# Attention in couples of query groups by Strassen's seven block products, with array halves that swap PSUM banks

## The chip, the cores and the metric

The kernel runs on one core of one Trainium2 chip. The metric is the device time of one execution in microseconds (us); lower is better. Every kernel was run several times, each time beside runs of the kernel before on the same chip. On one core a run is put down as slow when it is over 1.5% above the fastest of the same kernel; only fast runs are compared here. Profiled spans are some 2 us shorter than the device time of the same run.

In the profile PE is TensorE, PEld its weight loads, DVE VectorE, ACT ScalarE, POOL GpSimd and SP SyncE. "SPq" is SP's sequencer, which issues the DMA transposes. L199 is line 199 of the kernel named.

## The reference, cut to what matters

```python
# u, v: (8, 3072, 256), z: (8, 3072, 64); w1, w2: (256, 1024), w_out: (1024, 256)
scores = z @ z^T / 3072                     # symmetric
x      = u * (max(scores, 0) ** 2 @ v)      # per batch
g      = maximum(x @ w1, x @ w2)
out    = g @ w_out                          # float32
```

A batch has 24 tiles of 128 tokens. The kernels work on groups of four tiles (512 queries), so a batch has six groups and its squared-relu matrix is 6 by 6 blocks of 512 by 512. The matrix is symmetric: a block above the diagonal is computed, the one below is its transpose, made by a DMA transpose ("mirror").

## The kernel before

One query group's attention is 48 steps: 24 key tiles times two halves of the output width. Each step is two matmuls of 64 rows by 512 columns, one in each half of the array. Each half adds into a bank of its own, and the two banks are merged afterwards (`drain`).

```python
def attn_unit(b, g, t, acc, dc, first, last):          # one step
    blk, j = divmod(t, G)
    a = A[b, g, blk]
    for half in range(2):
        rows = ds(half * R, R)                         # R = 64
        ...                                            # (cut: natural or mirrored block)
        nc.tensor.matmul(o, v_sb[b][rows, t, ts(dc, P)], mv, start=first, stop=last)

def drain(acc, dcs):                                   # merge the halves
    ...
        nc.scalar.copy(hs[dc], acc[1, dc])
    for dc in dcs:
        nc.vector.tensor_add(hs[dc], hs[dc], acc[0, dc])

def mirror(b, g, blk):                                 # block below the diagonal
    t = tpool.tile([P, G, G, P], bf16, name="at_sb")
    nc.sync.dma_start_transpose(t..., A[b, g, blk]...)
    A[b, blk, g] = t

def turn_u(b, g):
    t = upool.tile([P, G, KD, P], bf16, name="uT")
    nc.sync.dma_start_transpose(t..., un[b, g]...)     # z likewise (zT)

def gate(b, g, hs):                                    # DVE: xT = c2 * h * uT, two of 128x512
    ...

def ff1(xT, g_sb):
    for nb in range(KF):                               # eight slices of the first projection
        ...                                            # two matmuls into d_ps
        if nb % 2 == 0:
            nc.scalar.activation(g_sb[:, nb, :], d_ps, AF.Relu)
        else:
            nc.vector.tensor_single_scalar(out=g_sb[:, nb, :], in_=d_ps, scalar=0.0, op=ALU.max)
```

The feed-forward has been folded beforehand: max(a, b) = b + relu(a - b), so one projection with w1 - w2 and a product with w2·w_out are left. Attention and feed-forward of two groups alternate on TensorE.

Of the kernel before, what the change touches and what calls it, by code (L numbers as in the profile page):

```python
# [11 lines left out]
def kernel(  # L12
# [25 lines left out]
    NG = NT // G  # L38
    KD = D // P
    KF = Dff // P  # L40
    AHEAD = 11
    c2 = float((1.0 / S) * (1.0 / S))


    consts = ctx.enter_context(tc.tile_pool(name="consts", bufs=1))
    znat = ctx.enter_context(tc.tile_pool(name="znat", bufs=1))
    zpool = ctx.enter_context(tc.tile_pool(name="zpool", bufs=2))
    vpool = ctx.enter_context(tc.tile_pool(name="vpool", bufs=2))
    unat = ctx.enter_context(tc.tile_pool(name="unat", bufs=2))
    upool = ctx.enter_context(tc.tile_pool(name="upool", bufs=3))  # L50
    apool = ctx.enter_context(tc.tile_pool(name="apool", bufs=11))
    tpool = ctx.enter_context(tc.tile_pool(name="tpool", bufs=13))
    rpool = ctx.enter_context(tc.tile_pool(name="rpool", bufs=3))
    hpool = ctx.enter_context(tc.tile_pool(name="hpool", bufs=4))
    xpool = ctx.enter_context(tc.tile_pool(name="xpool", bufs=4))
    gpool = ctx.enter_context(tc.tile_pool(name="gpool", bufs=2))
# [8 lines left out]
    zn, zd, zT, v_sb, un, uT = {}, {}, {}, {}, {}, {}  # L65

    def load_z(b, lo, n, held=False):
        if b not in zn:
            zn[b] = znat.tile([P, NT, dqk], bf16, name="zn")
            zd[b] = znat.tile([P, NT, 2, dqk], bf16, name="zd")  # L70
            zT[b] = zpool.tile([P, NT, P], bf16, name="zT")
        sl = ds(lo, n)
        if held:
            nc.vector.memset(zn[b][:, lo, 0:1], 0.0)
        nc.gpsimd.dma_start(out=zn[b][:, sl, :], in_=by_tile(z[b])[:, sl, :])

    def first_z(lo, n):

        if 0 not in zd:
            zd[0] = znat.tile([P, NT, 2, dqk], bf16, name="zd")  # L80
            zT[0] = zpool.tile([P, NT, P], bf16, name="zT")
        t = tpool.tile([P, n, dqk], fp32, name=f"z32_{lo}", tag="at_sb")
        nc.sync.dma_start(out=t, in_=by_tile(z[0])[:, ds(lo, n), :])
        return t

    def double_first(t, lo, n, at=0, copies=None):
        for copy, h in zip(copies or (nc.vector.tensor_copy, nc.scalar.copy), range(2)):
            copy(zd[0][:, ds(lo, n), h, :], t[:, ds(at, n), :])

    def double_z(b, lo, n):  # L90
        sl = ds(lo, n)
        for h in range(2):
            nc.vector.tensor_copy(zd[b][:, sl, h, :], zn[b][:, sl, :])

    def zT_dma(b):
        nc.sync.dma_start_transpose(zT[b], zd[b].rearrange("p t h d -> p (t h d)"))

    def zT_pe(b, lo, n, engine):
        tp = mm_psum.tile([P, n, P], bf16, name="tpz", tag="mm")
        for j in range(n):  # L100
            nc.tensor.transpose(
                tp[:, j, :], zd[b][:, lo + j, :, :].rearrange("p h d -> p (h d)"), ident
            )
        copy = nc.scalar.copy if engine == "act" else nc.vector.tensor_copy
        copy(zT[b][:, lo : lo + n, :], tp)

    def load_v(b, lo, n, held=False):
        if b not in v_sb:
            v_sb[b] = vpool.tile([P, NT, D], bf16, name="v_sb")
        sl = ds(lo, n)  # L110
        if held:

            nc.vector.memset(v_sb[b][:, lo, 0:1], 0.0)  # L113
        nc.gpsimd.dma_start(out=v_sb[b][:, sl, :], in_=by_tile(v[b])[:, sl, :])  # L114
# [12 lines left out]

    A = {}
    later = []
    whole_first = (0, NG - 1)  # L130
    V_ORDER = (1, 2, 3, 4, 5, 0)
    V_LATE = [(3, 14), (4, 8), (4, 14), (5, 2), (5, 8), (5, 14)]

    def score_pair(b, g, m, dve_half=None, halves=False):
        blk = m // 2
        if m % 2 == 0:
            A[b, g, blk] = apool.tile([P, G, GW], bf16, name="a_sb")
        a = A[b, g, blk]
        k = 2 * (m % 2)

        triangle = blk == g and whole_first < (b, g)
        lo = [(k + h) * P if triangle else 0 for h in range(2)]
        s_ps = []
        for h in range(2):
            rows = ds(h * R, R)
            s_ps.append(mm_psum.tile([P, GW], fp32, name="s_ps", tag="mm"))
            nc.tensor.matmul(  # L147
                s_ps[h][:, lo[h] :],
                zT[b][rows, 2 * m + h, :],
                zT[b][rows, g * G + lo[h] // P : g * G + G, :].rearrange("p t c -> p (t c)"),  # L150
                start=True,
                stop=True,
            )
# [7 lines left out]
        if halves or triangle:  # L161
            for h in range(2):
                o = r[:, h, lo[h] :]
                nc.vector.tensor_mul(a[:, k + h, lo[h] :], o, o)  # L164
        else:
            nc.vector.tensor_mul(a[:, k : k + 2, :], r, r)  # L166
        if triangle and m % 2 == 1:
            for j in range(G - 1):
                nc.sync.dma_start_transpose(
                    a[:, j + 1 :, ts(j, P)], a[:, j, (j + 1) * P :]  # L170
                )
        if m % 2 == 1 and blk > g:
            if b == 0 and g < 2 and blk > 2:
                later.append((b, g, blk))
            else:
                mirror(b, g, blk)

    def mirror(b, g, blk):

        t = tpool.tile([P, G, G, P], bf16, name="at_sb")  # L180
        nc.sync.dma_start_transpose(
            t.rearrange("p k j r -> p (k j) r"),
            A[b, g, blk].rearrange("p k q -> p (k q)"),
        )
        A[b, blk, g] = t



    def attn_unit(b, g, t, acc, dc, first, last):
        blk, j = divmod(t, G)  # L190
        a = A[b, g, blk]
        for half in range(2):
            rows = ds(half * R, R)
            if blk >= g:
                o, mv = acc[half, dc], a[rows, j, :]
            else:
                o = acc[half, dc].rearrange("p (k r) -> p k r", r=P)
                mv = a[rows, :, j, :]
            nc.tensor.matmul(o, v_sb[b][rows, t, ts(dc, P)], mv, start=first, stop=last)  # L199

    def drain(acc, dcs):
        hs = {}
        for dc in dcs:
            hs[dc] = hpool.tile([P, GW], fp32, name="h_sb")
# [5 lines left out]
    def drain_fast(acc, dc):  # L210

        hs = [hpool.tile([P, GW], fp32, name="h_sb") for half in range(2)]
# [3 lines left out]

    def gate(b, g, hs):
        xT = xpool.tile([P, KD, GW], bf16, name="xT")
        for dc in range(KD):
            nc.vector.scalar_tensor_tensor(  # L220
                out=xT[:, dc, :].rearrange("p (t r) -> p t r", r=P),
# [6 lines left out]
        return xT  # L228

    def ff1(xT, g_sb):  # L230
        for nb in range(KF):
# [9 lines left out]
            if nb % 2 == 0:  # L241
                nc.scalar.activation(g_sb[:, nb, :], d_ps, AF.Relu)  # L242
            else:
# [3 lines left out]

    def ff2(b, g, xT, g_sb, last=False):
        dst = by_tile(out[ds(b * S, S), :])[:, ds(g * G, G), :]
        o_sb = opool.tile([P, G, D], fp32, name="o_sb")  # L250
        for t0 in range(0, G, 2):
            o_ps = mm_psum.tile([P, 2, D], fp32, name="o_ps", tag="mm")
            for t in range(2):
# [16 lines left out]
            nc.scalar.copy(o_sb[:, t0 : t0 + 2, :], o_ps)  # L270
            if last:
                nc.sync.dma_start(out=dst[:, ds(t0, 2), :], in_=o_sb[:, t0 : t0 + 2, :])
        if not last:
            nc.sync.dma_start(out=dst, in_=o_sb)
# [7 lines left out]


    def ff_follows(i):
        return i >= 2 and i % 2 == 0 or i == len(groups) - 1

    def edge(i):

        return 0 if ff_follows(i) else 4 if i < 2 else 9
# [9 lines left out]
    def pair_slots(i):  # L299
        if i == 0:  # L300
            return [1, 3] + list(range(6, 40, 4))
        if i == 1:
            return list(range(3, 41, 4))
        if ff_follows(i):
            return [3, 9, 15, 21, 26, 31, 36, 40]
        return [0, 5, 10, 15, 20, 25, 30, 41]



    groups = [(b, g) for b in range(B) for g in range(NG)]  # L310

    def tiles_of(b, g):
        own = list(range(g * G, g * G + G))
        rest = list(range(g * G + G, NT))
        return list(range(g * G)) + (own + rest if (b, g) <= whole_first else rest + own)

    pairs, need = [], {}
    for i, (b, g) in enumerate(groups):
        order = [(b, g, m) for m in range(2 * g, NT // 2)]
        base = len(pairs)  # L320
        pairs += order
        most = base
        for n, t in enumerate(tiles_of(b, g)):
            if t // G >= g:
                most = max(most, base + order.index((b, g, t // 2)) + 1)
            need[i, n] = most

    done = 0

    def ahead(upto):  # L330
        nonlocal done
        while done < min(upto, len(pairs)):
            early = done < 22
            score_pair(
                *pairs[done],
                dve_half=1 if early and done % 3 == 0 else None,
                halves=done == 0,
            )
            done += 1

    def ff(prev):
        g_sb = gpool.tile([P, KF, GW], bf16, name="g_sb")
        ff1(prev[2], g_sb)
        return g_sb

    with tc.manual_schedule():
        z32a = first_z(0, 4)
        z32b = first_z(4, 8)
        z32c = first_z(12, 12)
        warm = consts.tile([P, GW], bf16)  # L350
# [156 lines left out]
```

## Time and profile before

| | before |
|---|---|
| device time | 969.06 us (968.63 to 970.68, 3 runs) |
| profiled span | 966.4 us |
| attention, all stretches on TensorE | 583.5 us |
| feed-forward, all stretches on TensorE | 377.8 us |
| one batch, steady | 118.2 us |
| attention of two groups, steady | 24.17, 23.96 or 22.88 us, mean 23.67 |
| feed-forward of two groups | 15.75 us |

The stretches are worked out from the start times of the matmuls in the trace: a stretch runs from its first matmul to the first one of the other kind.

The page of the kernel before has these lines (busy us and share by engine; busy tenths in 40 slices for PE and the DMA engines; the chain that ended last; two groups, with busy us and mean ns of one; block transposes with the median us from issue to landing):

```profile
PE 954.8 (99%) x7994; PEld 621.6 (64%) x8042; DVE 487.2 (50%) x847; ACT 557.6 (58%) x1058; POOL 61.0 (6%) x118
...
PE   8999999999999999999999999999999999999998
...
DMA  9999798988689976999869988699967998767611
...
PE 96%; DVE 1%; issue 1%; ACT 1%; DMA 1%; DVEq 0%; POOLq 0%
...
L244 DVE TENSOR_SCALAR g_sb<-d_ps 128x512 bf16<-128x512 f32 x192 | 132.8, 692 | 146.1 <-PE d_ps L234 146.1
...
at_sb<-a_sb SPq DMA_TRANSPOSE x120, 5.0
```

TensorE is busy 99% of the span and is 96% of the chain; DVE idles half of the time. TensorE's longest waits, from the waits view (us in total, times, longest):

```profile
PE acc_134 L374 <- DVE warm L351: 1.2, 1, 1.2
PE acc_427 L199 <- DVE a_sb L166: 1.1, 3, 0.5
```

There is nothing longer than 1.2 us in the whole run. The windows view of the start (length, busy us of PE, PEld, DVE, ACT and POOL, then granted clock, DMA share, GB/s) reads:

```profile
0.00:60.00 60.00, 54.97 (x465) 27.82 (x467) 40.67 (x68) 41.73 (x75) 12.59 (x27) 1.00 1.10 182
60.00:100.00 40.00, 39.90 (x338) 24.03 (x338) 22.15 (x39) 25.88 (x49) 2.65 (x5) 1.00 1.11 199
100.00:160.00 60.00, 59.84 (x506) 37.31 (x508) 27.69 (x49) 33.91 (x65) 3.71 (x7) 1.00 0.86 152
```

After the first 60 us TensorE is never short of work. A DMA share of 1 or just over it is to be read as "full".

### The profile page before, as it was taken

How to read it: one execution, taken by the hardware profiler on the slowest of the kernel's cores; microseconds unless marked ns; L12 is line 12 of the kernel's file. 1: busy time of each engine (PE TensorE's matmuls, PEld its weight loads, DVE VectorE, ACT ScalarE, POOL GpSimd, SP SyncE). 2: the span in 40 equal slices, each digit the busy share in tenths (PEclk: the TensorE clock that was granted, in tenths of full speed). 3: DMA queues.
4: the chain of work that ended last, by engine and by line, in shares of the span. 5: the costliest groups of instructions: out<-in, count | busy, mean ns of one | idle time of the engine just before them, and what ended most of it. 6: DMA issues, size and time to landing. Idle time of an engine off the chain costs nothing.

```text
span 966.4 us, 19478 instructions
## 1 busy us (share of the span) xinstructions
PE 954.8 (99%) x7994; PEld 621.6 (64%) x8042; DVE 487.2 (50%) x847; ACT 557.6 (58%) x1058; POOL 61.0 (6%) x118
## 2 busy tenths in 40 slices
PE   8999999999999999999999999999999999999998
PEld 4465667675666756667566765676756776566655
DVE  6746454463555534555346553464545554445433
ACT  6757466563575645756456564565556656466433
POOL 3001000100000000000000000000000000000000
PEclk9999999999999999999999999999999999999999
DMA  9999798988689976999869988699967998767611
GB/s 186 186 207 175 135 156 158 179 149 166 134 140 188 146 157 126 164 185 148 150 133 146 184 152 160 131 162 176 150 141 140 157 170 168 135 131 145 124 56 44
DMA packets 382296, 145.99 MB, mean 151 GB/s; under 512 B 360832, under 2 KB 361984, under 8 KB 382208
## 3 DMA queue, kind: packets, MB, share of 16 engines
q1 hardware_dynamic: 365792, 115.25, 62.5%
q0 software_dynamic: 16416, 29.50, 20.8%
q8 instruction: 63, 1.03, 0.4%
q14 instruction: 25, 0.20, 0.1%
HBM read 59.77 MB, written 25.17 MB: 88 GB/s over the span
## 4 chain that ended last, share of the span: by engine, by line
PE 96%; DVE 1%; issue 1%; ACT 1%; DMA 1%; DVEq 0%; POOLq 0%
PE o_ps L263 17%; PE d_ps L234 17%; PE s_ps L147 7%; PE o_ps L255 4%; DMA v_sb<-in_v_dram 1%; DVE a_sb L166 1%; PE acc_12604 L199 1%; PE acc_6354 L199 1%; PE acc_4771 L199 1%; PE acc_3187 L199 1%; PE acc_11103 L199 1%; PE acc_9519 L199 1%; PE acc_7936 L199 1%; PE acc_1582 L199 1%; PE acc_1581 L199 1%
## 5 line engine op out<-in xcount | busy, mean ns | idle before, releaser
L199 PEld LDWEIGHTS <-v_sb 64*128 64x128 bf16 x4608 | 314.6, 94 | 181.4 <-issue 5.9
L160 ACT ACTIVATE r_sb<-s_ps 128x512 bf16<-128x512 f32 (+3 forms) x664 | 333.8, 555 | 90.4 <-PE s_ps L147 88.8
L166 DVE TENSOR_TENSOR a_sb<-r_sb 128x1024 bf16<-128x1024 bf16 x251 | 173.6, 692 | 243.0 <-ACT r_sb L160 239.0
L244 DVE TENSOR_SCALAR g_sb<-d_ps 128x512 bf16<-128x512 f32 x192 | 132.8, 692 | 146.1 <-PE d_ps L234 146.1
L263 PE MATMUL o_ps<-w_out_sb,g_sb 128*128 128x256 bf16 x1536 | 199.1, 273 | 0.0
L234 PE MATMUL d_ps<-xT,w_sb 128*128 128x512 bf16 x720 | 167.4, 379 | 2.6 <-issue 0.2
L263 PEld LDWEIGHTS <-g_sb 128*128 128x128 bf16 x1536 | 150.2, 98 | 20.8
L242 ACT ACTIVATE g_sb<-d_ps 128x512 bf16<-128x512 f32 x192 | 114.8, 598 | 82.0 <-PE d_ps L234 57.1
L147 PE MATMUL s_ps<-zT 64*128 64x512 bf16 (+3 forms) x672 | 148.6, 357 | 0.9 <-DVE r_sb L158 0.5
L270 ACT COPY o_sb<-o_ps 128x512 f32<-128x512 f32 x96 | 56.3, 586 | 150.3 <-PE o_ps L263 149.2
L234 PEld LDWEIGHTS <-w_sb 128*128 128x128 bf16 x768 | 73.2, 98 | 89.6 <-issue 9.8
L255 PE MATMUL o_ps<-W2o_sb,xT 128*128 128x256 bf16 x384 | 73.3, 273 | 0.0
L118 POOL DMA_DIRECT2D un<-in_u_dram x48 | 25.7, 537 | 731.2 <-DMA uT<-un 717.6
L147 PEld LDWEIGHTS <-zT 64*128 64x128 bf16 x672 | 47.6, 94 | 29.0 <-issue 4.6
L220 DVE SCALAR_TENSOR_TENSOR xT<-h_sb,uT 128x512 bf16<-128x512 f32 x96 | 61.8, 685 | 0.0
L164 DVE TENSOR_TENSOR a_sb<-r_sb 128x512 bf16<-128x512 bf16 (+3 forms) x170 | 47.9, 323 | 14.7 <-ACT r_sb L160 14.5
L255 PEld LDWEIGHTS <-xT 128*128 128x128 bf16 x384 | 37.6, 98 | 14.1
L114 POOL DMA_DIRECT2D v_sb<-in_v_dram x48 | 25.8, 546 | 59.1 <-DVE v_sb L113 58.3
L199 PE MATMUL acc_134<-a_sb,v_sb 64*128 64x512 bf16 x24 | 8.7, 377 | 0.5 <-DMA v_sb<-in_v_dram 0.4
L199 PE MATMUL acc_136<-a_sb,v_sb 64*128 64x512 bf16 x24 | 8.7, 378 | 0.0
L199 PE MATMUL acc_137<-a_sb,v_sb 64*128 64x512 bf16 x24 | 8.5, 376 | 0.0
L199 PE MATMUL acc_135<-a_sb,v_sb 64*128 64x512 bf16 x24 | 8.5, 376 | 0.0
(577 smaller groups left out, 1665.3 us busy)
## 6 DMA issues: line engine op xcount, KB each, us to landing
out_dram<-o_sb SPq DMA_DIRECT2D x47, 512.0 KB, 4.0
v_sb<-in_v_dram POOLq DMA_DIRECT2D x48, 256.0 KB, 7.0
un<-in_u_dram POOLq DMA_DIRECT2D x48, 256.0 KB, 5.0
zn<-in_z_dram POOLq DMA_DIRECT2D x7, 384.0 KB, 6.7
a_sb<-a_sb SPq DMA_TRANSPOSE x126, 2.7
at_sb<-a_sb SPq DMA_TRANSPOSE x120, 5.0
uT<-un SPq DMA_TRANSPOSE x48, 3.3
w_132<-in_moe_w_dram POOLq DMA_DIRECT2D x1, 512.0 KB, 5.1
```

Source lines behind the costliest of these rows:

```text
L147: nc.tensor.matmul(s_ps[h][:, lo[h] :], zT[b][rows, 2 * m + h, :], zT[b][rows, g * G + lo[h] // P : g * G + G, :].rearrange("p t c -> p (t ...
L160: nc.scalar.activation(o, s, AF.Relu)
L164: nc.vector.tensor_mul(a[:, k + h, lo[h] :], o, o)
L166: nc.vector.tensor_mul(a[:, k : k + 2, :], r, r)
L199: nc.tensor.matmul(o, v_sb[b][rows, t, ts(dc, P)], mv, start=first, stop=last)
L220: nc.vector.scalar_tensor_tensor(out=xT[:, dc, :].rearrange("p (t r) -> p t r", r=P), in0=hs[dc].rearrange("p (t r) -> p t r", r=P), scala ...
L234: nc.tensor.matmul(d_ps, w15_sb[:, kc, ts(nb, P)], xT[:, kc, :], start=(kc == 0), stop=(kc == KD - 1),)
L242: nc.scalar.activation(g_sb[:, nb, :], d_ps, AF.Relu)
L244: nc.vector.tensor_single_scalar(out=g_sb[:, nb, :], in_=d_ps, scalar=0.0, op=ALU.max)
L255: nc.tensor.matmul(o_ps[:, t, :], xT[:, dc, ts(t0 + t, P)], W2o_sb[:, dc, :], start=(dc == 0), stop=False,)
L263: nc.tensor.matmul(o_ps[:, t, :], g_sb[:, nb, ts(t0 + t, P)], w_out_sb[:, nb, :], start=False, stop=(nb == KF - 1),)
L270: nc.scalar.copy(o_sb[:, t0 : t0 + 2, :], o_ps)
```

## The change

Two query groups become a couple; a batch has three couples. For the blocks of a couple that lie off the couple's diagonal, the 2 by 2 block product (two query groups by two key groups, times two key groups by two halves of v's width) is done with Strassen's seven products (in Winograd's form) for eight. The couple's own four blocks are done plainly. That is 7 x 8 + 4 x 8 = 88 steps for a couple where 2 x 48 = 96 stood. Four forms of A and four of v are needed: S1 to S4 are sums of whole 128x2048 blocks, the forms of v smaller.

A bank now holds one product, with both halves of the array added into it: the halves work on different products, and swap. An order between the halves is kept by no-ops on POOL (the prediction's relays). So nothing is merged, but the products have to be added up (U2, U3, V), on DVE.

In batch 0 the first four groups stay plain (`PLAIN = 4`), so 22 couples take the new form. The core of the diff, with cuts marked `...`:

```diff
+    PLAIN = 4
...
-    apool = ctx.enter_context(tc.tile_pool(name="apool", bufs=11))
-    tpool = ctx.enter_context(tc.tile_pool(name="tpool", bufs=13))
+    free = [apool.tile([P, G * GW], bf16, name=f"blk{n}") for n in range(NSLOTS)]   # 27
-    hpool = ctx.enter_context(tc.tile_pool(name="hpool", bufs=4))
+    hpool = ctx.enter_context(tc.tile_pool(name="hpool", bufs=5))
...
+    def prepare(b, c):                       # DVE: three block sums for each of two couples
+        ...
+                nc.vector.tensor_add(f["S1"].ap, f["A21"].ap, f["A22"].ap)
+                nc.vector.tensor_sub(f["S2"].ap, f["S1"].ap, f["A11"].ap)
+                nc.vector.tensor_sub(f["S3"].ap, f["A11"].ap, f["A21"].ap)
+    ORDER = (                                # what each half of the array works on, in turn
+        (("P1", "P6", "P7", "X11"), ("X11", "P1", "P6", "P7")),
+        (("D22", "X12", "P5", "X21"), ("P5", "X21", "D22", "X12")),
+    )
+    BANK = {"P1": 0, "P6": 1, "P7": 2, "X11": 3, "D22": 0, "P5": 1, "X21": 2, "X12": 3}
...
-            if nb % 2 == 0:
-                nc.scalar.activation(g_sb[:, nb, :], d_ps, AF.Relu)
-            else:
+            if nb in (2, 5, 7):
                 nc.vector.tensor_single_scalar(...)
+            else:
+                nc.scalar.activation(g_sb[:, nb, :], d_ps, AF.Relu)
+            hook(1, nb)                      # DVE tasks are put between the relus
...
-        if not last:
-            nc.sync.dma_start(out=dst, in_=o_sb)
+            nc.scalar.copy(o_sb, o_ps)       # two stores of 256 KB for one of 512
+            nc.sync.dma_start(out=dst[:, ds(t0, 2), :], in_=o_sb)
...
+    return forms, list(gates) + sums[:3] + tasks + sums[3:]     # order of DVE's tasks
...
+                (50, lambda: turn_u(b, q1)),                     # u of a couple, at steps 50 and 60
+                (60, lambda: turn_u(b, q2)),
...
+                    if (s, half) in marks:
+                        relay = nc.gpsimd.nop()
+                        tc.add_manual_dep(relay.ins, mm.ins.name, AFTER, reason="half done")
```

All off-diagonal blocks of both groups of a couple must be there, in their mirrored form where they lie below the diagonal, before the couple's block sums can be made. And the gates of the couple just attended stand first in the list of DVE's work for the feed-forward that follows, which is that of the couple before it.

## The prediction

> **What bounds the kernel now.** TensorE. The page's busy table gives PE 99%, against ACT 58% and DVE 50% of a 966.4 us span; the chain of waits is 96% PE; the granted clock is 1.000. In the timeline, the feed-forward of two groups takes 15.75 us, the attention of two groups 22.9 to 24.2 us, and each couple of half-array matmuls (64 rows, 512 columns, one in each half) starts 0.2155 us after the last. Sum per batch: 118.25 us, of which 3 x 96 x 0.2155 = 62.1 us are attention products, 8.9 us scores, 47.25 us feed-forward. The Trainium skill, "TensorEngine Tiling (Array Packing)", Key Properties, says that row tiles run independently; the trace agrees, as two matmuls of 0.38 us start within 0.01 to 0.11 us of each other.
>
> **What the change removes.** Off the diagonal, seven products replace eight: 88 steps per couple of groups instead of 96, in 22 couples (the first four groups of batch 0 stay plain). 22 x 8 x 0.2155 = 37.9 us of TensorE, all on the critical path. ACT evictions of accumulators fall from 88 to 44; one relu of eight goes from DVE to ACT.
>
> **What it adds.** DVE, per couple: eight sums of 128x2048 bf16 (the one in the trace took 1.219 us; about 1.13 start to start, estimated from 0.60 for 1024), eight 512-wide fp32 additions where four were (0.60 us start to start), and about four 512-wide V sums (0.34). Per batch I estimate 46 us of DVE issue in the attention stretches and 46 in the feed-forward, 92 of about 114 us: 81%, from some 45%. DMA work stays (share 0.85 to 0.9 in the windows table). The half-swap relays through POOL have at least eight steps (1.7 us) of slack, so they should cost nothing; two halves never write one bank at once, as the same skill page's Gotcha 1 demands (no run here tests that).
>
> **What is given back.** In the feed-forward DVE is as loaded as TensorE. After attention, DVE first does two final additions and a gate before the first relu that ff1 needs, and the third relu comes late for the second projection: an estimated 0.3 us of TensorE wait per couple, and 0.3 more in one couple of three where a 1.2 us block sum stands between relus of the second group. That is some 9 us over the run, in place of nearly none now. The plain start and DVE queueing behind transposes: 3 to 5 us more.
>
> **Predicted time:** 969 - 38 + 13 = 944 us, 8 in 10 between 935 and 960. Chances: faster by over 2% 0.69, within 2% 0.28, slower 0.03.
>
> **What would show it.** 176 steps of two matmuls fewer (7994 recorded matmuls down by about 350); attention stretches of two groups 1.7 us shorter; feed-forward stretches 16.0 to 16.6 us instead of 15.75, the gap before the second projection released by a DVE relu; DVE busy near 80%; PE still above 97% and the chain of waits still mostly PE; steps of two matmuls still 0.2155 us apart.
>
> **What would make it wrong.** DVE's queue runs later than I think (block sums waiting for transposes that read the block they overwrite, gates waiting for the u transpose), so that attention waits for sums or relus: 960 or more. Half-array matmuls of different products failing to overlap (steps over 0.22 us) would cancel the gain. If DVE's slack suffices everywhere, 935.

## More of the kernel before

All transposes stand in one stream, SP's, in program order. They have to: the Trainium skill, "DMA: Bandwidth & Descriptors", section "Silent corruption: two transposing streams in flight at once", says that two streams whose transposes are in flight together can corrupt each other's output. No run here tests that; both kernels and every experiment keep to it.

## The result, and the profile after

| | before | after |
|---|---|---|
| device time, median | 968.88 us (968.63 to 970.68, 4 runs) | 955.26 us (954.55 to 955.75, 4 runs) |
| profiled span | 966.4 us | 952.7 us |
| attention, all stretches | 583.5 us | 556.2 us |
| feed-forward, all stretches | 377.8 us | 391.6 us |
| one batch, steady | 118.2 us | 113.9 us |
| attention of a couple, steady | mean 23.67 us | 21.48, 22.12, 21.80, mean 21.80 us |
| feed-forward of a couple, steady | 15.75 us | 15.96 us mostly, up to 17.07 |

The ratio is 0.9856 (95% interval 0.9842 to 0.987). Here and below a ratio is the mean time of one kernel's fast runs over that of the other's of the same rounds, so not quite the ratio of the medians quoted. The changed kernel is 1.4% faster: inside the predicted range, 11 us above its centre, and in the class "within 2%" that the prediction held for less likely. All results were correct.

The page after:

```profile
PE 926.9 (97%) x7690; PEld 519.1 (54%) x7690; DVE 731.9 (77%) x1180; ACT 551.9 (58%) x1062; POOL 57.2 (6%) x111
...
PE   8968979999999999999999999999999999999998
...
DMA  9998996989898897887958989689899989884401
...
PE 89%; DMA 4%; DVE 4%; SPq 1%; issue 1%; ACT 1%; DVEq 0%; ACTq 0%; POOLq 0%
...
L403 DVE TENSOR_SCALAR g_sb<-d_ps 128x512 bf16<-128x512 f32 x144 | 96.2, 684 | 27.1 <-PE d_ps L395 23.3
...
L311 DVE TENSOR_TENSOR blk<-blk,blk 128x2048 bf16<-128x2048 bf16 x44 | 53.8, 1223 | 1.3
...
blk<-blk SPq DMA_TRANSPOSE x246, 5.0
```

DVE went from 50% to 77%. (The 246 transposes are 120 of blocks and 126 of triangles of diagonal blocks, as before, where they have two names. The median of 5.0 us is of both kinds here; in the trace the 120 of blocks alone have 6.0 us, against 5.0 in the kernel before.) The row of slices shows where TensorE is not full: the third, the fourth and the sixth, that is, before 143 us. The waits view of TensorE agrees:

```profile
PE s_ps L201 <- DMA zT<-zd: 9.1, 1, 9.1
PE d_ps L395 <- DVE g_sb L403: 4.6, 3, 3.9
PE s_ps L201 <- ACT o_sb L431: 1.7, 2, 1.3
...
PE o_ps L423 <- DVE g_sb L403: 0.8, 4, 0.2
```

Three waits that the kernel before doesn't have stand out, and the longest case of each (9.1, 3.9 and 1.3 us) lies in the start. The windows view of the changed kernel cuts the run there:

```profile
60.00:64.60 4.60, 4.60 (x44) 2.18 (x40) 3.44 (x7) 4.60 (x10) 0.00 (x0) 1.00 0.82 180
64.60:73.70 9.10, 0.03 (x2) 0.00 (x0) 1.25 (x4) 0.27 (x1) 0.53 (x1) 0.65 1.05 199
73.70:78.70 5.00, 4.96 (x28) 1.69 (x28) 1.40 (x3) 2.27 (x5) 1.59 (x3) 0.62 1.13 210
60.00:163.50 103.50, 88.66 (x717) 49.15 (x714) 72.92 (x122) 58.66 (x116) 5.84 (x11) 0.93 0.92 160
163.50:882.50 719.00, 716.72 (x5990) 401.70 (x5990) 584.35 (x941) 422.77 (x820) 38.15 (x72) 1.00 0.90 159
```

From 163.5 us on TensorE is busy 716.7 of 719 us. Between 60 and 163.5 us it is busy 88.7 of 103.5 us, and it also runs slower after the two longer holes: the clock granted was 0.65 in the hole of 9.1 us and 0.62 in the 5 us after it. By the Trainium skill, "TensorE: Matmul & The Clock Gate", Part 1, about 3.4 us of idleness bring the clock to half and about 3.4 us of work bring it back. The trace agrees in size: the clock is at half from 67.26 to 77.50 us, that is, from 2.6 us after the last matmul's end until 3.8 us after work goes on, and again from 125.29 to 128.70 us, after the second hole; the third and shortest hole has no such stretch. So the two longer holes cost more than their length.

**The first hole** (64.6 to 73.7 us). The chain of waits of the changed kernel, in this window alone, shows what TensorE waited for (start us, us, what):

```profile
63.55 0.24 PE s_ps L201 x2
63.79 0.72 SPq L243
...
64.61 2.01 SPq L177
...
66.72 3.60 SPq L243
...
70.42 3.27 DMA zT<-zd
...
73.74 0.61 PE s_ps L201 x2
74.35 1.71 PE acc L259 x5
```

The last plain group has finished batch 0's scores, and its slots emit two pairs of score matmuls of batch 1. These need batch 1's z, turned. The transpose (L133) stands behind a transpose of u (L177) and block transposes (L243) in SP's stream. From 35.87 to 64.5 us SP issues nine block transposes, one every 3.2 us, without a pause. TensorE has work of batch 0 ready but works in program order.

**The second hole** (120.8 us, 4.25 us without a matmul start; this feed-forward takes 21.50 us instead of 15.75). DVE's lines in the timeline (start, length, idle before it and its releaser):

```profile
123.69 0.69 DVE L379 SCALAR_TENSOR_TENSOR xT<-h_sb,uT 128x512 bf16<-128x512 f32 x1 [3.69 <-DMA uT<-un]
124.29 0.68 DVE L403 TENSOR_SCALAR g_sb<-d_ps 128x512 bf16<-128x512 f32 x1
```

The gate waits for u, turned by a transpose that was issued at 115.61 and landed only at 123.66 us, between block transposes issued at 113.13 and 117.31 us. The relu that TensorE needs stands behind the gate on DVE.

**The third hole** (141.2 to 143 us). A score matmul needs a PSUM bank which ACT empties; ACT waits for an output buffer. Its store was ready when ACT's copy, begun at 129.5 us, had ended; SP issued it at 138.18 us, after block transposes at 129.58, 131.63 and 136.36 us, and it landed at 142.19 us. ACT's waits of this kind in the whole run (the longest, 6.9 us, is this one; the six others come later):

```profile
ACT o_sb L431 <- DMA out_dram<-o_sb: 21.2, 7, 6.9
```

The sum of it, all from the stretches. Twenty-two couples at 1.87 us less (23.67 - 21.80) should take 41.1 us from attention; it lost 27.3 us. The missing 13.8 us lie in the plain start (12.8 us longer than in the first experiment, which takes the first hole away) and in the couple with the third hole (2.2 us over its steady 21.80); these come to 15.0 us, so the other stretches won 1.2 us more than the count. The feed-forward grew by 13.9 us: 6.2 us in its first two stretches (16.16 and 21.50), 7.7 us in all the others together. So the start gave back about 20 us, the steady feed-forward about 8.

### The profile page after: what moved, and what is told of

Same layout as the page of the kernel before. It is cut to its first block, busy times and chain, and to the rows that moved or that the text cites. A ratio compares the mean times of both kernels' runs of the same rounds, so it can differ in the third digit from the quotient of the medians.

```text
span 952.7 us, 19447 instructions
## 1 busy us (share of the span) xinstructions
PE 926.9 (97%) x7690; PEld 519.1 (54%) x7690; DVE 731.9 (77%) x1180; ACT 551.9 (58%) x1062; POOL 57.2 (6%) x111
## 2 busy tenths in 40 slices
DMA packets 388651, 145.99 MB, mean 153 GB/s; under 512 B 361936, under 2 KB 365904, under 8 KB 388560
## 4 chain that ended last, share of the span: by engine, by line
PE 89%; DMA 4%; DVE 4%; SPq 1%; issue 1%; ACT 1%; DVEq 0%; ACTq 0%; POOLq 0%
PE acc L789 44%; PE o_ps L423 17%; PE d_ps L395 15%; PE s_ps L201 6%; PE o_ps L415 4%; PE acc L259 3%; DMA uT<-un 2%; DVE g_sb L403 1%; DVE blk L303 1%; DVE blk L222 1%; DMA blk<-blk 1%; SPq L243 1%; DVE xT L379 1%; DMA v_sb<-in_v_dram 1%; DMA out_dram<-o_sb 0%
## 5 line engine op out<-in xcount | busy, mean ns | idle before, releaser
L789 PE MATMUL acc<-blk,v_sb 64*128 64x512 bf16 x2464 | 465.4, 376 | 0.0
L789 PE MATMUL acc<-blk,vt 64*128 64x512 bf16 x1408 | 345.0, 376 | 0.0
L789 PEld LDWEIGHTS <-v_sb 64*128 64x128 bf16 x2464 | 182.9, 94 | 136.5 <-issue 4.6
L222 DVE TENSOR_TENSOR blk<-r_sb 128x1024 bf16<-128x1024 bf16 x251 | 170.8, 689 | 106.4 <-ACT r_sb L214 104.8
L789 PEld LDWEIGHTS <-vt 64*128 64x128 bf16 x1408 | 131.4, 94 | 74.0 <-issue 0.6
L201 PE MATMUL s_ps<-zT 64*128 64x512 bf16 (+3 forms) x672 | 126.9, 358 | 11.6 <-DMA zT<-zd 9.1
L706 DVE TENSOR_TENSOR h_sb<-h_sb,acc 128x512 f32<-128x512 f32 x154 | 101.5, 682 | 28.7 <-PE acc L789 27.9
L403 DVE TENSOR_SCALAR g_sb<-d_ps 128x512 bf16<-128x512 f32 x144 | 96.2, 684 | 27.1 <-PE d_ps L395 23.3
L220 DVE TENSOR_TENSOR blk<-r_sb 128x512 bf16<-128x512 bf16 (+3 forms) x170 | 50.7, 323 | 35.1 <-ACT r_sb L214 34.2
L259 PE MATMUL acc<-blk,v_sb 64*128 64x512 bf16 x384 | 52.1, 385 | 2.9 <-DVE blk L222 1.2
L311 DVE TENSOR_TENSOR blk<-blk,blk 128x2048 bf16<-128x2048 bf16 x44 | 53.8, 1223 | 1.3
L307 DVE TENSOR_TENSOR blk<-blk,blk 128x2048 bf16<-128x2048 bf16 x44 | 53.6, 1217 | 0.0
```

Of the source, the lines that this page charges most:

```text
L201: nc.tensor.matmul(s_ps[h][:, lo[h] :], zT[rows, z_at(b, blk * G + tiles[h]), :], zT[rows, q + lo[h] // P : q + G, :].rearrange("p t c -> ...
L222: nc.vector.tensor_mul(a[:, k : k + 2, :], r, r)
L259: nc.tensor.matmul(a.out(acc[half, dc]), v_at(b, t, dc)[rows], a.moving(rows, j), start=first, stop=last,)
L706: nc.vector.tensor_add(out, a, b_)
L789: mm = nc.tensor.matmul(a.out(acc[name]), w()[rows], a.moving(rows, j), start=name not in opened, stop=left[name] == 0,)
```

## The experiments

Three theories stood at the outset. By the first, the three holes are three separate mistakes of order, and each one taken away gives its length back. By the rival (B, called the transposes in flight, their bandwidth, or the amount of DMA work), the delivery of the transposes limits the start: what waits changes when a wait is taken away, not when they come. By a third, DVE's order in the feed-forward (gates and sums before relus) is what costs, and it should be changed for all batches. Where the expectations use letters for theories, they say beside them what each expects. The first four kernels ran on one chip with one set of runs of the kernel before (median 968.66 us).

### 1. No scores of batch 1 in the plain start

```diff
-                while done < min(upto, len(pairs)):
+                while done < min(upto, per_batch):
```

> Edit: the plain start emits score pairs of batch 0 only, so TensorE does not stop at 64.6 us for the z transpose of batch 1. Theory A (a score pair placed too early waits in order for a transpose that stands behind others in the SP queue): the 9.1 us hole and the half-clock stretch after it (5 us at granted clock 0.62) vanish, 943 to 948 us against 955.3. Rival B (the transposes in flight are the limit, so TensorE only waits elsewhere, at the block sums or the u gates): the hole is gone but waits after it grow, 951 to 955 us.

Measured: 958.52 us (953.97 to 962.49), ratio 0.9895 (0.9861 to 0.9929). The first hole is gone and the plain stretch is 64.70 us instead of 77.52. But the next two feed-forward stretches took 21.17 and 27.41 us. TensorE's waits:

```profile
PE d_ps L395 <- DVE g_sb L403: 13.4, 5, 5.3
PE s_ps L201 <- ACT o_sb L431: 2.2, 2, 1.9
```

The attention of batch 1's first couple begins at 138.03 us, against 139.47 in the changed kernel, so 1.4 of 12.8 us are kept at that point, and the median is no better. The windows view of this kernel:

```profile
60.00:100.00 40.00, 36.30 (x290) 20.60 (x290) 28.80 (x53) 23.79 (x49) 2.64 (x5) 0.96 1.01 170
100.00:160.00 60.00, 48.82 (x393) 28.61 (x393) 40.69 (x65) 31.33 (x64) 2.64 (x5) 0.94 0.82 147
```

The time went over to the gates that wait for u. (The profile is of the fastest of the four runs.) Between 100 and 160 us the DMA share is 0.82 while TensorE idles, so the bytes that the DMA engines can move are not the whole limit.

### 2. The first couple's u turned first

```diff
+        for q in range(2):
+            load_u(0, PLAIN + q)
...
-                (50, lambda: turn_u(b, q1)),
-                (60, lambda: turn_u(b, q2)),
+                (0 if early else 50, lambda: turn_u(b, q1)),     # early: the first couple alone
+                (0 if early else 60, lambda: turn_u(b, q2)),     # (its loads at steps 2 and 6 fall away)
```

> Edit: in the first couple by seven products (batch 0) the two u transposes are issued at its first step instead of steps 50 and 60, ahead of the block transposes in the SP queue. Theory A (queue order: the gates wait for u transposes that were issued last): the 3.9 us hole in the feed-forward at 121 us and the half clock after it vanish, 949 to 951 us. Rival B (transpose bandwidth): the wait moves to the output writes or the block sums, 954 to 955.5 us.

Measured: 955.5 us (953.42 to 956.62), ratio 0.9863 (0.9848 to 0.9877). The second hole is gone (that feed-forward takes 16.39 us). The third has grown:

```profile
PE s_ps L201 <- DMA zT<-zd: 9.2, 1, 9.2
PE s_ps L201 <- ACT o_sb L431: 6.3, 1, 6.3
```

The feed-forward after batch 1's first couple begins at 165.28 us, against 163.46 in the changed kernel.

### 3. Both

The edits of 1 and 2 together.

> Edit: both of the foregoing. Theory A: 937 to 942 us, the two savings add up and the steady batches (113.9 us each) stay as they are. Rival B: what is saved at the start is lost again before the third couple, 948 us or more.

Measured: 953.54 us (950.0 to 959.13), ratio 0.9842 (0.9795 to 0.9889). The first feed-forward has a hole of 8.33 us (a transpose of u landed 12.1 us after its issue), and a wait for the store takes 9.0 us. That feed-forward begins at 165.93 us.

### 4. Batch 1's first z turned early

```diff
-                if (i, n) in ((2, 6), (2, 20)):
+                if (i, n) in ((1, 6), (2, 20)):        # load
-                if (i, n) in ((3, 4), (3, 8)):
-                    turn_z(1, int(n == 8))
+                if (i, n) in ((2, 2), (3, 8)):         # transpose
+                    turn_z(1, int(i == 3))
```

> Edit: the early score pairs of batch 1 stay, but the z piece that they read is loaded and transposed a group and a half earlier, so that its transpose stands before some six block transposes in the SP queue. Theory A (order in the queue, not the amount of work): the 9.1 us hole goes, 943 to 949 us. Rival B (amount of work): the block transposes pushed back by it hold TensorE instead, 952 us or more.

Measured: 957.55 us (947.64 to 961.11), ratio 0.987 (0.9815 to 0.9925). The wait for z is gone; in its place, in TensorE's waits:

```profile
PE d_ps L395 <- DVE g_sb L403: 11.1, 2, 10.7
PE s_ps L201 <- ACT o_sb L431: 4.0, 4, 2.2
PE acc L259 <- DMA blk<-blk: 3.9, 1, 3.9
```

What follows from 1 to 4: each edit removed the wait it was made for, and none moved the median by more than 4 us. Whichever waits were taken away, the feed-forward after batch 1's first couple began at 162.6 to 167.9 us in the runs profiled. So the three holes do not simply add up: what was freed at one was mostly lost at the next. But each kernel has one profile, and their runs spread far more (8 to 13 us in 1, 3 and 4) than those of the changed kernel (1.2 us). Experiment 4 had a run of 947.64 us and experiment 3 two of 950.0 and 950.7, against 954.55 for the best of the changed kernel; their profiles are of slower runs (958.66 and 956.38 us). In some runs, then, a part of the time taken away seems to have been kept; no profile shows where.

### 5. Gates last, no DVE task between the relus of the first projection

```diff
-            return forms, list(gates) + sums[:3] + tasks + sums[3:]
+            return forms, sums[:3] + tasks + sums[3:] + list(gates)
-            places = {(1, 0): 1, (1, 3): 1, (2, 0): 1, (2, 1): 1, (2, 2): 1, (2, 3): 1}
+            first = {(2, 0): 1, (2, 1): 1, (2, 2): 1}       # first group of the couple
+            places = (first, {(2, 0): 100})                 # second group: the rest
```

This and the next three ran on one chip (kernel before: 969.28 us).

> Edit: in the feed-forward of every couple DVE gets no block sum and no gate between the relus of the first projection, and the gates come last of its list. Theory B (the first 146 us are held by the DMA engines, share 1.0 to 1.2, and a wait taken away comes back at the next consumer): only the steady gain of 0.2 to 0.4 us per feed-forward, some 5 us, so 948 to 952 us. Theory C (the late u transpose costs only because the gate stands before the relus in DVE's order): the 3.9 us hole and its half clock go as well, 942 to 947 us. Steady feed-forward 15.75 us in both.

Measured: 1025.61 us (1023.33 to 1026.94), ratio 1.0571 (1.0537 to 1.0606): slower. Every feed-forward from the first on of two groups took 15.74 to 15.84 us, so the DVE order is what costs 0.2 to 1.3 us in the changed kernel's feed-forward. But attention lost much more. From the waits view, TensorE's, ACT's and SP's line:

```profile
PE s_ps L201 <- ACT o_sb L431: 63.6, 16, 10.9
...
ACT o_sb L431 <- DMA out_dram<-o_sb: 127.0, 16, 16.5
...
SPq L133 <- DVE blk L222: 47.0, 7, 12.0
```

The list of DVE's tasks ends, in both forms, with the copies of z that precede the transpose of z. Now they come late, SP stands at that transpose (L133), and the stores behind it in SP's program order are late by as much. ACT can't free its output buffers, so it doesn't empty the banks that the next scores need.

### 6. The same without scores of batch 1 in the plain start

The edits of 1 and 5.

> Edit: gates last and no early score pairs of batch 1. Theory B: the block sums or the output writes hold TensorE before 146 us for as long as the two holes did, 946 to 952 us. Theory C: 936 to 941 us, both holes gone.

Measured: 1012.11 us (1009.67 to 1014.35), ratio 1.0442 (1.0405 to 1.048). Feed-forward 15.75 us in all but one couple (16.47); of TensorE's waits nearly all are again for the stores:

```profile
PE s_ps L201 <- ACT o_sb L431: 61.7, 17, 10.1
```

### 7. All of batch 0 plain

```diff
-    PLAIN = 4
+    PLAIN = 6
```

The loads, the z transposes and the slots of the score pairs were moved to suit, and the first two feed-forwards were put after the third group.

> Edit: all six groups of batch 0 by plain products, two feed-forwards after the third group as in the kernel before; seven products from batch 1 on (21 couples instead of 22, 1.7 us more TensorE work). Theory B: the transposes are needed later, TensorE is busy while they run, 935 to 943 us and steady batches unchanged; this would show that the start, not the seven products, gave the gain back. If the transposes hold it all the same: 950 us or more.

Measured: 960.77 us (957.54 to 965.66), ratio 0.991 (0.9863 to 0.9956). One couple fewer in the new form costs 1.9 us, estimated from the steady stretches; the median rose by 5.5 us. The holes are still there when the couples begin with batch 1: one feed-forward took 23.02 us (a gap of 6.17 us, gate waiting for u), and TensorE waited 5.9 us for ACT's output copies and 2.4 us for z. So what collides is not the end of the plain code as such, but the first couples after it, wherever they are.

### 8. No loads of v for batch 1 (wrong on purpose)

```diff
+        if b == 1:
+            vp[b, piece] = vp[0, piece]
+            return
```

Batch 1 is attended with batch 0's v; the relative error is 0.43.

> Edit, wrong result on purpose: batch 1 uses the v tiles of batch 0, so 3.1 MB of loads between 76 and 125 us are gone and nothing else moves. Theory B (amount of DMA work): holes at 121 and 141 us shrink by most of their 6 us, and the hole at 64.6 us, before these loads, stays: 946 to 950 us. Theory A (order in the SP queue alone): 954 to 956 us.

Measured: 953.56 us (953.29 to 956.27), ratio 0.9837 (0.9806 to 0.9868). The second hole is nearly gone (16.99 us), a hole of 1.86 us for the store stays, and the wait for z, before those loads matter, was longer in this run:

```profile
PE s_ps L204 <- DMA zT<-zd: 13.4, 1, 13.4
```

With three loads of 512 KB fewer (as the page counts them), the DMA share from 100 to 160 us fell from 0.94 to 0.78. Contention with these loads is a part of what makes the transposes slow there: the transpose of u that the gate waits for took 5.18 us from issue to landing, in place of 8.05. But the feed-forward also began 3.2 us later, after the longer first hole, so not all of the shrinking of the second hole is due to the loads. It is not the part that the first hole waits for, and the fixed point of experiments 1 to 4 came at 162.23 us, 1.2 us earlier.

### 9 and 10. Stores off SP's stream

If stores are late because they stand behind transposes, another engine's queue should free them. Both start from experiment 6. This pair ran on a chip of its own (kernel before: 968.74 us).

```diff
-            nc.sync.dma_start(out=dst[:, ds(t0, 2), :], in_=o_sb)
+            nc.gpsimd.dma_start(out=dst[:, ds(t0, 2), :], in_=o_sb)      # 10: nc.scalar
```

> Edit: as e6_gates_last_no_early (gates last, no early score pairs), and the output stores are issued by POOL instead of SP, so that they no longer stand behind block transposes. In e6 the feed-forwards took 15.75 us each and all of TensorE's 62 us of recorded waits were for ACT copies that waited for a store to free o_sb. Theory D (not the amount of DMA work, but what stands behind the transposes in the one SP queue: first u and z transposes, then the stores): those waits go, 920 to 932 us. Theory B (amount of DMA work in the first 150 us): the time comes back as waits of block sums or gates for DMA, 945 us or more.

> Edit: the same with the stores issued by ACT, whose queue also holds the copies. Theory D: the same gain less what the issuing costs ACT (96 issues, 0.33 us each on SP): 922 to 938 us. Theory B: 945 us or more. If e12 is slow and this is not, the POOL relays of the half swap were held behind the stores.

Measured for POOL's queue: 983.88 us (979.04 to 988.79), ratio 1.0154 (1.0107 to 1.0201). Compared with experiment 6, on another chip, that is 28 us less. The waits for the stores went from 61.7 to 1.8 us, and the transposes of z took their place:

```profile
PE s_ps L201 <- DMA zT<-zd: 31.1, 10, 13.6
PE acc L791 <- DVE blk L727: 3.9, 1, 3.9
PE s_ps L201 <- ACT o_sb L431: 1.8, 2, 1.5
```

The z copies still come last on DVE. The feed-forward after batch 1's first couple began at 155.72 us here (in a profile of the slowest of the four runs), 7.7 us earlier than in the changed kernel, with nearly the same transposes issued by then (38 of blocks and triangles against 39, 7 of u against 8, 3 of z in both) and no stores among them. Measured for ACT's queue: 980.42 and 992.96 us in its two fast runs, ratio 1.0183 (1.0107 to 1.0259); two more, of 999.6 and 1010.24 us, were slow. Its profile was of a slow run, and nothing is read from it.

### 11 and 12. The copies of z first on DVE

Experiment 11 is experiment 9 with the copies of z at the head of DVE's tasks; 12 is the same with the stores back on SP (kernel before: 968.95 us).

```diff
-        second(PLAIN // 2 - 2, tasks + [lambda: turn_z(1, 2)])
+        second(PLAIN // 2 - 2, [lambda: turn_z(1, 2)] + tasks, 1)
...
-                    tasks += [
+                    turns = [
                         lambda piece=piece: turn_z(b + 1, piece) for piece in ((0, 1), (2,))[c]
                     ]
+                tasks = turns + tasks
```

> Edit: as e12 (gates last, no early score pairs, stores on POOL), and the DVE copies that a z transpose waits for come first of DVE's list of a feed-forward instead of last. In e12 31 of TensorE's 40 us of recorded waits were score products waiting for a z transpose that SP could issue only after those late copies. Theory D (what waits is what stands late in an in-order list, on DVE or SP): these go, with the half clock after them, 932 to 945 us; left is the hole at 142 us, a block sum waiting for a block transpose. Theory B (amount of DMA work): 960 us or more.

> Edit: the same with the stores on SP as in the changed kernel. Theory D': in e5 and e6 the stores were late because SP stood at a z transpose that waited for the late DVE copies, so with the copies first the stores come in time in the steady batches too: 932 to 948 us, and every feed-forward 15.75 us. If the stores stand behind the block transposes whatever the z copies do (as I held for e12): 970 us or more, with waits of score products for ACT's o_sb copies.

Experiment 11 measured 954.58 us (950.66 to 960.36), ratio 0.9856 (0.9816 to 0.9896). The windows view:

```profile
65.00:162.50 97.50, 82.59 (x666) 46.30 (x662) 67.89 (x114) 53.44 (x106) 9.72 (x18) 0.93 0.94 154
162.50:875.00 712.50, 712.50 (x5994) 402.87 (x5993) 585.13 (x943) 421.79 (x821) 80.27 (x148) 1.00 0.88 161
```

From 162.5 us on TensorE never waits: the feed-forward takes 15.75 us and the couples 21.48, 22.12 and 21.80 us each time, 112.6 us for a batch. Before that it waits as long as the changed kernel did (15 us in both), in other places again. A copy of z on DVE now waits for its load, with the relus behind it, and a block sum waits for a block transpose:

```profile
PE d_ps L395 <- DVE g_sb L403: 9.6, 2, 9.0
PE acc L791 <- DVE blk L727: 5.4, 1, 5.4
```

Its time hides a part of the gain. TensorE's last matmul ended at 940.5 us, 8.5 us earlier than in the changed kernel (949.0), yet the span is only 1.9 us shorter. After the last stores a DRAIN instruction on POOL takes from 941.46 to 950.02 us, and the program ends 10.3 us after the last matmul, where the changed kernel takes 3.7. There POOL has no stores, and its DRAIN (8.16 us) is over by 920.80 us. With the last stores alone back on SP this kernel could be some 6.6 us faster, an estimate from these two ends; it was not run.

Experiment 12 measured 969.03 us (965.7 to 970.88), ratio 0.9999 (0.9973 to 1.0026). With the stores on SP the steady waits for them are back, though z is early. One store was ready at 124.10 us and issued at 140.30, after a transpose of u and four of blocks with hardly a pause between them:

```profile
PE s_ps L201 <- ACT o_sb L431: 20.4, 11, 8.2
```

So with gates last the late copies of z were only one part of the trouble: the block transposes themselves hold up the stores too. With the gates late the stores need a queue of their own, or time is lost. The other half, stores on their own queue with the gates first, was not run.

How the twelve expectations fared: no gain that was expected came. Experiments 2, 3, 4 and 7 ended in the ranges that go with time coming back elsewhere. Experiments 9 and 10 did so by their numbers, but by other waits than were expected (for z). Experiments 1, 5 and 6 were slower than every range, 8 and 11 fell between the ranges, and 12 (969.03 us) just missed "970 us or more", with the waits that were named beside it.

### The stream of transposes, counted

To compare the two kernels at the same number of groups done: at 163.46 us the changed kernel has attended eight groups and passed four through the feed-forward. The kernel before has done as much at an estimated 144.9 us (its state of nine and six groups at 172.66 us, less one feed-forward of two groups, 15.75 us, and about 12.0 us for one group's attention). Counted in the trace up to there, what SP had issued:

```
                        before, to 144.9 us     after, to 163.46 us
block transposes                21                      27
triangle transposes              6                      12
transposes of u                  8                       8
transposes of z                  1 (a whole batch)       3 (a third each)
output stores                    5                       8
time spent issuing            99.8 us                124.6 us
SP's share issuing, 28-60 us   0.96                    0.92
                    90-120 us  0.55                    0.75
                   120-150 us  0.53                    0.76
```

In both kernels SP does little but issue between 28 and 60 us. The kernel before then catches up. The changed one has issued six block transposes and six triangles more by this point. It has also computed more scores (156 score matmuls against 118 in the trace of the kernel before at that time), because the next couple needs all its blocks at once, where single groups need them a group at a time. That is 25 us more of issuing. How long SP is held by one block transpose is no fixed cost, though: 1.33 to 7.65 us in the changed kernel and up to 9.65 us in experiment 3. Whether SP or the DMA engines behind it set this time, no run separates. The Trainium skill, "Perfetto Trace Analysis", section "What 'DMA-bound' means", names this case, a DMA sequencer that is solid with issues, beside that of full DMA engines. The trace agrees for 28 to 60 us (0.92 in the changed kernel, 0.97 in experiment 1); later shares are 0.75 to 0.81 in the changed kernel, which leaves room, so there the order within the stream is the likelier cause; in experiment 1 the stream is full again from 90 to 120 us (0.96).

## Why the prediction was right or wrong

- **"22 x 8 x 0.2155 = 37.9 us of TensorE, all on the critical path": right, and a little small.** The program emits 352 fewer accumulating matmuls (4,626 to 4,274 in the traces; the page's total falls by 304 only, because the trace before lacks 48 records of the first projection, 720 of 768). The steady stretch fell by 1.87 us where 1.72 was predicted; some 0.1 us of the rest is in the score matmuls, whose order also changed (the 84 of a batch take 8.1 us from start to start, in place of 8.4). The median step of two matmuls is 0.216 us in both kernels, so products of different kinds in the two halves overlap as equal ones did, and the relays cost nothing visible.
- **DVE near 80%: right.** The page says 77%, and 584.35 of 719 us in the steady windows is 81%, the figure that the prediction estimated for the batch.
- **"Feed-forward stretches 16.0 to 16.6 us, the gap before the second projection released by a DVE relu", some 9 us over the run: right.** 15.96 us mostly, and 16.18 us in one couple of three, where three stretches lie above the range (16.64, 16.94 and 17.07); 7.7 us outside the start. The waits view names the DVE relu (L403) for the second projection, and experiments 5 and 11 remove the loss by moving DVE's tasks.
- **"DMA work stays": right in the large.** 145.99 MB in both pages; the steady share is 0.90 in place of 0.85.
- **"The plain start and DVE queueing behind transposes: 3 to 5 us more": wrong, and this is the step that failed.** The start gave back about 20 us: 13.8 in attention, 6.2 in the feed-forward. The mechanism was named (under what would make it wrong: gates waiting for the transpose of u), but its size was put down, without a working, as if a wait in the start were as rare and short as in the kernel before, where TensorE has none over 1.2 us. The prediction did not ask how full SP's stream was (0.96 from 28 to 60 us), nor how many more transposes the couples need by the same point.
- **"PE still above 97% and the chain mostly PE": just right for the first (926.9 of 952.7 us), and the chain fell from 96% to 89%.** The missing 7 points are DMA, DVE and SPq, the start.
- **The time.** Put the measured terms in place of the predicted ones and the sum is 969 - 41 + 20 + 8 = 956 us, against 955.26 measured. With 4 us for the start it would have been 940. So the time fell inside the range because the range was 25 us wide: the start was some 16 us worse than predicted, and only some 4 us of that came back from the other terms.

What is shown: the three holes and what each waited for; that removing any of them, or two, moved waits on and, in the one profile of each, left the end of the start within 4.5 us of where it was; that loads of v are only a part; that the steady state can be had free of waits (experiment 11). What is argued from counts and not shown by a run of its own is that the larger number of transposes, rather than their order, fixes that end. Experiment 9 speaks against the number alone: nearly the same transposes, and the end 7.7 us earlier. No kernel with fewer block transposes in the start was run, so the shares of number, order and DMA load stay open. A kernel that is clearly better than the changed one was not found: 953.54 (experiment 3) and 954.58 us (experiment 11) have ranges that hold 955.26, experiment 11 with a longer end that eats most of what it wins before.

## What to carry to other kernels

Before counting a cut in the bounding engine's work as gain, count what the new form needs earlier: a form that takes its inputs in larger parcels moves the same transfers to the front, and the stream that issues them may already be full there although no wait shows it yet. When several waits hang on one in-order stream, removing one of them hands its time to the next, so judge an experiment by the time at which a fixed point of the program is reached, not by the wait that vanished, and look at the end too: moving stores to another queue can lengthen it (by 6.6 us in experiment 11). An order that is best on one engine (gates last on DVE) can be ruinous for a queue that takes its cue from that engine, unless what stands behind in that queue (here the stores) is moved off it.

## What the Trainium skill lacked or had wrong

- "DMA: Bandwidth & Descriptors" gives a bandwidth for DMA transposes and, beside its table for trn3, sequencer cycles on earlier chips, but no measured time that one holds its issuing engine on this chip, nor how that time varies. In the changed kernel, SP took a median of 2.37 us to issue a transpose of a 128x2048 bf16 block (1.33 to 7.65 us, 120 of them, 373.5 us in all) and 1.20 us for one of a diagonal block's triangle (126 of them, 172.1 us in all). From issue to landing the medians are 6.0 and 3.9 us.
- None of the pages looked up warns that output stores issued from the engine that issues transposes wait behind them. Here that came to 63.6 us of TensorE waits in experiment 5, and moving the stores to POOL's queue took experiment 6 from 1012.11 to 983.88 us.
- None of the pages looked up says that a program whose last DMAs are issued by POOL ends with a long DRAIN on that engine: 8.56 us in experiment 11.
- "TensorE: Matmul & The Clock Gate" gives 215.7 ns from start to start for one warm matmul of 512 columns, and no figure for two that share the array. Here two matmuls of 512 columns, one in each array half, start 0.216 us after the last two.
